# Splitting the dense attention's weights on ScalarE and VectorE in the middle of the last batch, and moving casts and gate copies of that batch to ScalarE

## The chip, the cores and the metric

One core of a Trainium2 chip runs the whole program. TensorE (PE) multiplies matrices, VectorE (DVE), ScalarE (ACT) and GpSimd (POOL) do everything else, and SyncE (SP) issues nearly all transfers. Each engine takes its instructions in the order in which they stand in its queue. The metric is device time in microseconds (us) of one execution, lower is better.

## The reference

Three layers follow each other for 4 batches of 576 positions: a sparse attention (8 heads of 64, half of them local, half strided), a gated feed-forward layer, and a dense causal attention with four experts of which two are used per position. The part around the change is the end of the second layer and the start of the third:

```
xk = mu_k * x + (1 - mu_k) * x_prev          # x_prev: x shifted by one position
xr = mu_r * x + (1 - mu_r) * x_prev
k  = max(xk @ w_k, 0)                         # 512 -> 1024
v  = (k * k) @ w_v                            # 1024 -> 512
r  = sigmoid(xr @ w_r)                        # 512 -> 512, the gate
y  = r * v
...
q, k, v = y @ wq[e], y @ wk[e], y @ wv[e]     # then causal softmax, @ wo[e], gated sum
```

## The kernel before, in words

Numbers are float32, and the products keep that precision by splitting. `split(src, h, l, he, le)` (L114) makes a rounded high part `h` on engine `he` and the rest `l = src - h` on engine `le`; a product is then three matmuls, high by high, high by low, low by high. The feed-forward layer of one batch, `p2_units(b)` (L451), works on two chunks of positions (320 and 256 columns). For a chunk, `prep` (L457) makes four pieces (one per 128 channels) of the mixed input for the gate (`xh_3_0`, `xl_3_0` of tag xh1) and four for the keys: POOL forms the difference `xd` (L472) once, DVE forms `xf = xd * mu + prev` (L479), and the split gives `xh` and `xl`. `mm3` (L536) makes four gate products `pr` of 12 matmuls and `evac` copies each from PSUM into the gate buffer `sg`; `mm1` (L500) makes eight key products `pk` of 12 matmuls, ACT does relu and square into `rf`, and a split gives `kk`; `mm2` (L554) makes four value products `pv` of 24 matmuls, and DVE multiplies each into `sg`, which is then written to memory (`x_spill`). One sigmoid over all of `sg` (L548) stands between the gate copies and the first of these multiplications.

`in_order` (L576) gives a batch's order: gate and key preparations and products of the first chunk, gate of the second, values of the first (`A["2"]`), then keys and values of the second (`Z["1"]`, `Z["2"]`). The batches overlap: while batch b is in its feed-forward layer, the sparse attention of batch b+1 is interleaved. The last batch (b = 3) has nothing to be interleaved with, so its feed-forward layer runs by itself between the last attention tiles and the dense attention. A list scheduler places the instructions of each engine within these dependences, so that an instruction can land earlier than its line in the text.

The PSUM tag `mm` has three banks that go round over `pr`, `pk` and `pv`. The fourth gate product needs the bank of the first, that is, the copy of the first into `sg`.

Just ahead of the last batch (L852 to L860) the four weights of the dense attention, 512 KB each (`wq`, `wk`, `wvg`, `wo`), are loaded one after the other into one staging buffer of tag `x2f`, and split: high part on ACT, low part on POOL. The buffer is free for the next load when POOL has made the low part. The same buffer then takes `x2f_0`, the first input chunk of the dense attention (L888), whose high part `x2h` is cast on ACT and whose low part `x2l` is made on DVE.

Of the kernel before, what the change touches and what calls it, by code (L numbers as in the profile page):

```python
# [7 lines left out]
F32 = mybir.dt.float32  # L8
# [8 lines left out]
P = 128  # L17
# [3 lines left out]
def interleave(main, side):  # L21

    tm = sum(c for c, _ in main) or 1.0
    ts_ = sum(c for c, _ in side) or 1.0
    im = is_ = 0
    am = as_ = 0.0
    while im < len(main) or is_ < len(side):
        if is_ < len(side) and (im >= len(main) or as_ / ts_ <= am / tm):  # L30
            c, f = side[is_]
            f()
            as_ += c
            is_ += 1
        else:
            c, f = main[im]
            f()
            am += c
            im += 1
# [3 lines left out]
def kernel(  # L43
# [19 lines left out]
    nc = tc.nc  # L63
    B, C, S = out.shape
# [3 lines left out]
    NKC = C // P  # L68
# [7 lines left out]
    CM = 320  # L76
# [11 lines left out]
    def ps_mm(name):  # L88
        return bank("mm", name, 3)
# [9 lines left out]
    def evac(dst, src, e=None):  # L99
        if e is None:  # L100
            flip["n"] += 1
            e = (nc.scalar, nc.vector)[flip["n"] % 2]
        if e is nc.scalar:
            nc.scalar.copy(dst, src)  # L104
        else:
            nc.vector.tensor_copy(dst, src)
# [7 lines left out]
    def split(src, h, l, he, le):  # L114

        if he is nc.scalar:
            nc.scalar.copy(h, src)  # L117
        else:
            he.tensor_copy(h, src)
        le.tensor_tensor(l, src, h.bitcast(F32), op=ALU.subtract)  # L120
# [10 lines left out]
    for nr in (7, 6):  # L131
        n = NN * nr
# [88 lines left out]
    sg = p2.tile([P, NKC, S], F32, tag="sg", name="sg", bufs=1)  # L221
# [229 lines left out]
    def p2_units(b):  # L451
        xT = xTs[b]
        parts = []
        for ci, (s0, N) in enumerate(CHUNKS1):
            st = {}

            def prep(which, kc, ci=ci, s0=s0, N=N, st=st, part=None):  # L457
                def f():
                    if part == 1:
                        st["low", which, kc]()  # L460
                        return
                    whole = b == 0 and which == 1
                    if kc == 0 and whole:
                        st["w"] = p2.tile([P, NKC, CM], F32, tag=("xh1", "xl1")[ci], name=f"xw{which}_{b}_{ci}", bufs=1)
                    elif kc == 0:
                        st["h", which] = p2.tile([P, NKC, CM], F32R, tag=f"xh{which}", name=f"xh{which}_{b}_{ci}", bufs=1)
                        st["l", which] = p2.tile([P, NKC, CM], F32R, tag=f"xl{which}", name=f"xl{which}_{b}_{ci}", bufs=1)
                    cur = xT[:, kc, 1 + s0:1 + s0 + N]
                    prv = xT[:, kc, s0:s0 + N]
                    if which == 1:  # L470
                        d = p2.tile([P, CM], F32, tag="xd", name=f"xd{b}_{ci}_{kc}", bufs=4)
                        (nc.vector if b == 0 else nc.gpsimd).tensor_tensor(d[:, :N], cur, prv, op=ALU.subtract)  # L472
                        st["d", kc] = d
                    d = st["d", kc]
                    if whole:
                        xf = st["w"][:, kc, :]
                    else:
                        xf = p2.tile([P, CM], F32, tag="xf", name=f"xf{which}_{b}_{ci}_{kc}")
                    nc.vector.scalar_tensor_tensor(  # L479
                        xf[:, :N], d[:, :N], mu[:, which, kc:kc + 1], prv, op0=ALU.mult, op1=ALU.add  # L480
                    )

                    he = nc.scalar if b == 0 else nc.vector
                    if whole:
                        return
                    h, l = st["h", which][:, kc, :N], st["l", which][:, kc, :N]
                    if part is None:
                        split(xf[:, :N], h, l, he, nc.vector)
                    else:
                        nc.scalar.copy(h, xf[:, :N])  # L490
                        st["low", which, kc] = lambda: nc.vector.tensor_tensor(
                            l, xf[:, :N], h.bitcast(F32), op=ALU.subtract
                        )
                return (0.0, f)

            U = {"r": [prep(1, kc) for kc in range(NKC)], "k": [prep(0, kc) for kc in range(NKC)]}
# [39 lines left out]
            def mm3(oc, ci=ci, s0=s0, N=N, st=st):  # L536
                def f():
                    xh, xl = st["h", 1], st["l", 1]
                    pm = ps_mm(f"pr{b}_{ci}_{oc}")
                    os_ = slice(oc * P, (oc + 1) * P)  # L540
                    for kc in range(NKC):
                        nc.tensor.matmul(pm[:, :N], wrh[:, kc, os_], xh[:, kc, :N], start=(kc == 0), stop=False)  # L542
                        nc.tensor.matmul(pm[:, :N], wrh[:, kc, os_], xl[:, kc, :N], start=False, stop=False)  # L543
                        nc.tensor.matmul(pm[:, :N], wrl[kc][:, os_], xh[:, kc, :N], start=False, stop=(kc == NKC - 1))  # L544
                    evac(sg[:, oc, s0:s0 + N], pm[:, :N], nc.vector)
                    if oc == NKC - 1 and ci == 1:

                        nc.scalar.activation(sg, sg, AF.Sigmoid)  # L548
                return (1.5 * N / 288, f)
# [26 lines left out]
    def in_order(parts):  # L576
        A, Z = parts
        return A["r"] + A["k"] + A["3"] + Z["r"] + A["1"] + Z["k"] + Z["3"] + A["2"] + Z["1"] + Z["2"]

    def behind(units):  # L580

        last = {}
        for i in nc.cur_bb.bb.instructions:
            last[i.engine] = i
        last = [last[e] for e in (nc.tensor.engine, nc.vector.engine, nc.scalar.engine, nc.sync.engine)]

        def wrap(f):
            def g():
                with ExitStack() as es:
                    for i in last:  # L590
                        es.enter_context(tc.issue_after(i))
                    f()
            return g
        return [(c, wrap(f)) for c, f in units]
# [21 lines left out]
    A, Z = p2_units(0)  # L616
# [202 lines left out]
    main = behind(A["2"][6:] + Z["1"])  # L819
# [20 lines left out]
    w3 = ctx.enter_context(tc.tile_pool(name="w3", bufs=1, side="right", reuse_waits="tile"))  # L840
    EP = E // 2
    wqh = w3.tile([P, NKC, E * D], F32R, tag="wqh", name="wqh")
    wql = w3.tile([P, NKC, E * D], F32R, tag="wql", name="wql")
    wkkh = w3.tile([P, NKC, E * D], F32R, tag="wkkh", name="wkkh")
    wkkl = w3.tile([P, NKC, E * D], F32R, tag="wkkl", name="wkkl")
    GV = E * D + E
    wvgh = w3.tile([P, NKC, GV], F32R, tag="wvgh", name="wvgh")
    wvgl = w3.tile([P, NKC, GV], F32R, tag="wvgl", name="wvgl")
    woh = w3.tile([P, EP, C], F32R, tag="woh", name="woh")
    wol = w3.tile([P, EP, C], F32R, tag="wol", name="wol")  # L850

    for src, h, l in ((wq, wqh, wql), (wk, wkkh, wkkl), (wvg, wvgh, wvgl)):  # L852
        n = src.shape[2]
        st = w3.tile([P, NKC, CM], F32, tag="x2f", name="w3st")
        nc.sync.dma_start(st[:, :, :n], src)
        split(st[:, :, :n], h, l, nc.scalar, nc.gpsimd)
    st = w3.tile([P, NKC, CM], F32, tag="x2f", name="wost")
    st = st.rearrange("p c n -> p (c n)")[:, :EP * C].rearrange("p (e n) -> p e n", e=EP)
    nc.sync.dma_start(st, wo)
    split(st, woh, wol, nc.scalar, nc.gpsimd)  # L860

    interleave(in_order(p2_units(B - 1)), [])
    r1.close()

    p3 = ctx.enter_context(tc.tile_pool(name="p3", bufs=2, reuse_waits="tile"))
# [234 lines left out]
    for b in range(B):  # L1100
# [4 lines left out]
        units = []  # L1105
# [103 lines left out]
```

## Time and profile before

| | |
|---|---|
| median of 3 runs | 582.27 us (582.23 to 584.96) |
| span of the profiled execution | 582.6 us |
| PE busy | 552.8 us, 95% of the span |
| DVE / ACT / POOL busy | 400.7 / 327.3 / 103.9 us |
| mean granted TensorE clock | 0.994 |
| chain that ended last | PE 75%, DVE 11%, ACT 5% |

The profiled execution has no time beside its span; that span stands 0.3 us over the median of the runs. In the profile a row of an instruction says when it started and how long it took. Matmuls are pipelined, so that the distance from start to start is their cost, not the duration in the row. The number in square brackets is the idle time of the engine just ahead, with what ended it.

### The profile page before, as it was taken

What the parts mean: (1) busy time and instruction counts of PE and PEld (TensorE: products, weight loads), DVE (VectorE), ACT (ScalarE), POOL (GpSimd) and SP (SyncE); (2) the same over time, 40 slices, a digit from 0 to 9 for tenths busy, and PEclk for the clock granted to TensorE, in tenths of its full rate; (3) what the DMA queues carried; (4) which work ended last, traced back from release to release, by engine and by line L of the source; (5) the groups of instructions that cost most, each with busy time, mean ns of one, the idle gap of its engine ahead of it and who ended that gap; (6) DMA issues with size and microseconds to landing.
All of it is one profiled execution on the core that took longest, in us unless ns stands there. A gap on an engine that the chain in (4) does not pass through costs nothing.

```text
span 582.6 us, 12015 instructions
## 1 busy us (share of the span) xinstructions
PE 552.8 (95%) x4408; PEld 500.2 (86%) x4408; DVE 400.7 (69%) x1366; ACT 327.3 (56%) x966; POOL 103.9 (18%) x151
## 2 busy tenths in 40 slices
PE   4889899989999999999997999999999999999987
PEld 3557788879999998999997999999988998898956
DVE  3897998768975476964467872336888874875862
ACT  4986878780345441445431352246775874775763
POOL 0000000101211021201114310076513142221000
PEclk9999999999999999999999899999999999999999
DMA  8872531323011223010202122054512250311102
GB/s 270 327 252 76 155 120 46 103 109 119 2 30 59 87 83 120 2 64 24 87 20 90 38 84 80 23 113 92 126 30 55 65 128 2 81 42 42 56 28 82
DMA packets 27519, 49.69 MB, mean 85 GB/s; under 512 B 3525, under 2 KB 22213, under 8 KB 26693
## 3 DMA queue, kind: packets, MB, share of 16 engines
q1 hardware_dynamic: 22340, 44.21, 22.9%
q0 software_dynamic: 5120, 4.72, 4.6%
q8 instruction: 34, 0.56, 0.4%
q14 instruction: 25, 0.20, 0.1%
HBM read 34.77 MB, written 9.44 MB: 76 GB/s over the span
## 4 chain that ended last, share of the span: by engine, by line
PE 75%; DVE 11%; ACT 5%; issue 2%; DVEq 0%; ACTq 0%
PE pk L506 6%; PE pv L563 6%; PE pk L507 5%; PE pk L508 5%; PE pv L565 5%; PE pv L564 5%; PE py L1064 4%; PE pt L1042 4%; PE pr L542 2%; PE s L1006 2%; PE pr L543 2%; PE pr L544 2%; PE pos L413 2%; PE s L1007 2%; PE pw L1080 2%
## 5 line engine op out<-in xcount | busy, mean ns | idle before, releaser
L506 PE MATMUL pk<-xh,wkh 128*128 128x320 f32 (+1 forms) x256 | 79.6, 312 | 3.8 <-ACT rf L510 2.7
L563 PE MATMUL pv<-kk,wvh 128*128 128x320 f32 (+1 forms) x256 | 76.4, 303 | 0.0
L507 PE MATMUL pk<-xl,wkh 128*128 128x320 f32 (+1 forms) x256 | 75.7, 296 | 0.0
L508 PE MATMUL pk<-xh,wkl 128*128 128x320 f32 (+1 forms) x256 | 75.6, 295 | 0.0
L564 PE MATMUL pv<-kk,wvh 128*128 128x320 f32 (+1 forms) x256 | 74.3, 293 | 0.0
L565 PE MATMUL pv<-kk,wvl 128*128 128x320 f32 (+1 forms) x256 | 73.9, 293 | 0.0
L510 ACT ACTIVATE rf<-pk 128x320 f32<-128x320 f32 (+1 forms) x64 | 25.9, 407 | 57.7 <-PE pk L508 45.0
L1017 ACT ACTIVATE pe<-pe,nm 128x384 f32<-128x384 f32 (+4 forms) x80 | 48.3, 606 | 12.4 <-DVE nm L1011 10.2
L506 PEld LDWEIGHTS pk<-xh,wkh 128*128 128x128 f32 x256 | 48.5, 190 | 7.8 <-ACT rf L510 3.8
L237 ACT ACTIVATE el<-el,nm 128x96 f32<-128x96 f32 x72 | 26.2, 366 | 45.1 <-DVE nm L232 44.6
L563 PEld LDWEIGHTS pv<-kk,wvh 128*128 128x128 f32 x256 | 47.7, 188 | 2.1 <-issue 0.3
L507 PEld LDWEIGHTS pk<-xl,wkh 128*128 128x128 f32 x256 | 48.6, 190 | 0.1
L508 PEld LDWEIGHTS pk<-xh,wkl 128*128 128x128 f32 x256 | 48.4, 189 | 0.1
L564 PEld LDWEIGHTS pv<-kk,wvh 128*128 128x128 f32 x256 | 47.9, 188 | 0.0
L565 PEld LDWEIGHTS pv<-kk,wvl 128*128 128x128 f32 x256 | 47.7, 188 | 0.1
L1011 DVE CUSTOM_DVE_ANT_0 pe<-s,mcau 128x384 f32<-128x384 f32 (+4 forms) x80 | 36.6, 479 | 10.4 <-PE s L1007 9.7
L104 ACT COPY aT<-pt 128x256 f32<-128x256 f32 (+3 forms) x96 | 33.4, 381 | 16.2 <-PE pt L1042 15.5
L1042 PE MATMUL pt<-ident,pe 128*128 128x128 f32 x240 | 37.9, 275 | 2.1 <-ACT aT L104 1.3
L568 DVE TENSOR_TENSOR sg<-pv,sg 128x320 f32<-128x320 f32 (+1 forms) x32 | 14.4, 457 | 32.8 <-PE pv L565 30.4
L237 ACT ACTIVATE es<-es,nm 108x108 f32<-108x108 f32 (+1 forms) x80 | 30.3, 383 | 8.8 <-DVE nm L232 8.8
L479 DVE SCALAR_TENSOR_TENSOR xf<-xd,mu,xT 128x320 f32<-128x320 f32 (+1 forms) x56 | 33.0, 600 | 3.3 <-POOL xd L472 3.3
L120 DVE TENSOR_TENSOR kk<-rf,kk 128x320 fp32r<-128x320 f32 (+1 forms) x64 | 31.1, 488 | 4.6 <-ACT kk L117 3.4
(162 smaller groups left out, 1565.0 us busy)
## 6 DMA issues: line engine op xcount, KB each, us to landing
qkv<-in_loc_dram SPq DMA_DIRECT2D x6, 1168.0 KB, 5.1
qkv<-in_strd_dram SPq DMA_DIRECT2D x6, 896.0 KB, 4.7
wraw<-in_w_k_dram SPq DMA_DIRECT2D x7, 512.0 KB, 6.5
qkv<-in_w_v_dram SPq DMA_DIRECT2D x5, 512.0 KB, 4.1
x_spill<-sg SPq DMA_DIRECT2D x16, 160.0 KB, 1.8
x2f<-x_spill SPq DMA_DIRECT2D x4, 640.0 KB, 4.5
out_dram<-ot SPq DMA_DIRECT2D x16, 160.0 KB, 1.8
wraw<-in_w_r_dram SPq DMA_DIRECT2D x4, 512.0 KB, 7.7
```

Source lines behind the costliest of these rows:

```text
L104: nc.scalar.copy(dst, src)
L237: nc.scalar.activation(eg, eg, AF.Exp, bias=nm[:np_, i:i + 1], scale=-1.0, accum_out=sm[:np_, i:i + 1],)
L479: nc.vector.scalar_tensor_tensor(xf[:, :N], d[:, :N], mu[:, which, kc:kc + 1], prv, op0=ALU.mult, op1=ALU.add)
L506: nc.tensor.matmul(pm[:, :N], wkh[:, kc, fs], xh[:, kc, :N], start=(kc == 0), stop=False)
L507: nc.tensor.matmul(pm[:, :N], wkh[:, kc, fs], xl[:, kc, :N], start=False, stop=False)
L508: nc.tensor.matmul(pm[:, :N], wkl[:, kc, fs], xh[:, kc, :N], start=False, stop=(kc == NKC - 1))
L563: nc.tensor.matmul(pm[:, :N], wvh[:, fc, os_], kh[:, :N], start=(fc == 0), stop=False)
L564: nc.tensor.matmul(pm[:, :N], wvh[:, fc, os_], kl[:, :N], start=False, stop=False)
L565: nc.tensor.matmul(pm[:, :N], wvl[:, fc, os_], kh[:, :N], start=False, stop=(fc == NFC - 1))
L1011: nc.vector.tensor_tensor_reduce(out=pe[:m, c0:c0 + n], in0=pm[:m, :n], in1=mask, scale=-0.125, scalar=(BIG if i == 0 else nm[:m, 2 * e:2 ...
L1017: nc.scalar.activation(pe[:m, :nk], pe[:m, :nk], AF.Exp, bias=last, scale=-1.0, accum_out=sm[:m, e:e + 1],)
L1042: nc.tensor.transpose(pt[:, kk * P:(kk + 1) * P], pe[:, c0:c0 + P], ident)
```

## The change

Three edits, all for the last batch. The high parts of the mixed inputs are cast on ACT and no longer on DVE. The gate products are copied out of PSUM by ACT and no longer by DVE. And the weights of the dense attention are loaded and split by a list of units (`w3_units`), interleaved with the last 24 units of the batch (`A["2"] + Z["1"] + Z["2"]`); each split comes in two halves, high on ACT and low on DVE, POOL has no part in it any more. The staging buffer is free for the next load when DVE has made the second half.

```diff
-                    he = nc.scalar if b == 0 else nc.vector
+                    he = nc.scalar if b in (0, B - 1) else nc.vector
...
-                    evac(sg[:, oc, s0:s0 + N], pm[:, :N], nc.vector)
+                    evac(sg[:, oc, s0:s0 + N], pm[:, :N], nc.scalar if b == B - 1 else nc.vector)
...
-    for src, h, l in ((wq, wqh, wql), (wk, wkkh, wkkl), (wvg, wvgh, wvgl)):
-        n = src.shape[2]
-        st = w3.tile([P, NKC, CM], F32, tag="x2f", name="w3st")
-        nc.sync.dma_start(st[:, :, :n], src)
-        split(st[:, :, :n], h, l, nc.scalar, nc.gpsimd)
...
-    interleave(in_order(p2_units(B - 1)), [])
+    def w3_units():
+        units = []
+        for src, h, l in ((wq, wqh, wql), (wk, wkkh, wkkl), (wvg, wvgh, wvgl), (wo, woh, wol)):
+            rows, n = src.shape[1:]
+            st = {}
+            def load(src=src, rows=rows, n=n, st=st):
+                t = w3.tile([P, NKC, CM], F32, tag="x2f", name="w3st")
+                st["w"] = t.rearrange("p c n -> p (c n)")[:, :rows * n].rearrange("p (c n) -> p c n", n=n)
+                nc.sync.dma_start(st["w"], src)
+            units.append((0.0, load))
+            for r in range(0, rows, rows // 2):
+                def part(r=r, rows=rows, h=h, l=l, st=st):
+                    rs = slice(r, r + rows // 2)
+                    split(st["w"][:, rs], h[:, rs], l[:, rs], nc.scalar, nc.vector)
+                units.append((1.0, part))
+        return units
+    A, Z = p2_units(B - 1)
+    main = in_order((A, Z))
+    n = len(main) - len(A["2"] + Z["1"] + Z["2"])
+    interleave(main[:n], [])
+    interleave(main[n:], w3_units())
```

The text puts the first load behind the gate products, but the scheduler still issues it where it stood, ahead of the last `x_spill` of batch 2 on SP. ACT's queue at the start of the last batch, before (`aTs` are the last transposes of the sparse attention, `rf_0_0` the first relu and square of the keys):

```order
284 L104 COPY aTs_3_0_3682<-pts_3_0_1_3687 126x252
285 L104 COPY aTs_3_1_3740<-pts_3_1_1_3746 108x324
286 L117 CAST wqh<-w3st 128x1024
287 L117 CAST wkkh<-w3st 128x1024
288 L510 ACTIVATE rf_0_0_3986<-pk_0_0_3973 128x320
```

And now, the same stretch of ACT's queue (`xh_3_0_3831` is the gate's input, `xh_3_0_3857` the keys'):

```order
289 L117 CAST xh_3_0_3831<-xf_3_0_3_3853 128x320
290 L117 CAST wqh<-w3st 128x512 x2
291 L117 CAST xh_3_0_3857<-xf_3_0_0_3859 128x320
292 L117 CAST xh_3_0_3857<-xf_3_0_1_3863 128x320
293 L104 COPY sg<-pr_0_0_3875 128x320
294 L104 COPY sg<-pr_0_1_3889 128x320
295 L104 COPY sg<-pr_0_2_3903 128x320
296 L117 CAST xh_3_0_3857<-xf_3_0_2_3867 128x320
297 L117 CAST xh_3_0_3857<-xf_3_0_3_3871 128x320
298 L117 CAST wkkh<-w3st 128x512 x2
299 L104 COPY sg<-pr_0_3_3917 128x320
```

The casts of the weights now stand among casts and copies that PE needs. DVE's queue at the same place, before:

```order
805 L479 SCALAR_TENSOR_TENSOR xf_3_0_1_3879<-xd_0_1_3855,mu,xT_2738 128x320
806 L479 SCALAR_TENSOR_TENSOR xf_3_0_2_3883<-xd_0_2_3861,mu,xT_2738 128x320
807 L119 CAST xh_3_0_3873<-xf_3_0_1_3879 128x320
808 L119 CAST xh_3_0_3873<-xf_3_0_2_3883 128x320
809 L120 TENSOR_TENSOR xl_3_0_3874<-xf_3_0_1_3879,xh_3_0_3873 128x320
810 L120 TENSOR_TENSOR xl_3_0_3874<-xf_3_0_2_3883,xh_3_0_3873 128x320
811 L106 COPY sg<-pr_0_0_3891 128x320
```

DVE's queue at that place now:

```order
798 L120 TENSOR_TENSOR xl_3_0_3832<-xf_3_0_3_3853,xh_3_0_3831 128x320
799 L120 TENSOR_TENSOR wql<-w3st,wqh 128x512
800 L479 SCALAR_TENSOR_TENSOR xf_3_0_1_3863<-xd_0_1_3839,mu,xT_2738 128x320
801 L120 TENSOR_TENSOR wql<-w3st,wqh 128x512
802 L120 TENSOR_TENSOR xl_3_0_3858<-xf_3_0_0_3859,xh_3_0_3857 128x320
803 L120 TENSOR_TENSOR xl_3_0_3858<-xf_3_0_1_3863,xh_3_0_3857 128x320
804 L479 SCALAR_TENSOR_TENSOR xf_3_0_2_3867<-xd_0_2_3845,mu,xT_2738 128x320
```

DVE no longer casts or copies here, and has the low halves of the weights in their place. The second place is ACT's queue around the second chunk's gate, before:

```order
303 L510 ACTIVATE rf_0_7_4116<-pk_0_7_4103 128x320
304 L117 CAST woh<-wost 128x1024
305 L514 ACTIVATE rf_0_7_4116<-rf_0_7_4116 128x320
306 L548 ACT_TABLE_LOAD
307 L548 ACTIVATE sg<-sg 128x2304
308 L117 CAST x2h_0_4578<-x2f_0_4576 128x1024
```

The same place now, with the four gate copies `sg<-pr_1_*` that DVE made before:

```order
323 L514 ACTIVATE rf_0_7_4100<-rf_0_7_4100 128x320
324 L104 COPY sg<-pr_1_0_4123 128x256
325 L117 CAST xh_3_1_4105<-xf_3_1_2_4115 128x256
326 L117 CAST x2h_0_4586<-x2f_0_4584 128x1024
327 L104 COPY sg<-pr_1_1_4137 128x256
328 L117 CAST xh_3_1_4105<-xf_3_1_3_4119 128x256
329 L104 COPY sg<-pr_1_2_4151 128x256
330 L104 COPY sg<-pr_1_3_4165 128x256
331 L548 ACT_TABLE_LOAD
332 L548 ACTIVATE sg<-sg 128x2304
```

`woh` has moved up ahead of `rf_0_6`, and `x2h_0`, which stood behind the sigmoid, stands ahead of the copy of `pr_1_1`.

## Rows read from the trace of the kernel before

**Rows 1.** Waits of PE from 48 us to the end: total, times, longest.

```profile
PE pr L542 <- DVE sg L106: 3.4, 1, 3.4
```

**Rows 2.** Busy time in stretches: length, PE, PEld, DVE, ACT, POOL, PEclk, DMA, GB/s.

```profile
315.00:320.00 5.00, 1.57 (x8) 1.31 (x7) 5.00 (x10) 0.45 (x1) 2.52 (x4) 0.79 0.33 105
320.00:325.00 5.00, 5.00 (x22) 5.00 (x21) 4.97 (x10) 0.60 (x1) 2.42 (x2) 0.53 0.09 13
```

**Rows 3.** Timeline of PE in the last batch: start, duration, instruction, idle before.

```profile
310.01 0.30 PE L542 MATMUL pr<-xh,wrh 128*128 128x320 f32 x1
...
315.14 0.30 PE L544 MATMUL pr<-xh,wrl 128*128 128x320 f32 x1
318.87 0.64 PE L542 MATMUL pr<-xh,wrh 128*128 128x320 f32 x1 [3.43 <-DVE sg L106]
...
324.64 0.35 PE L506 MATMUL pk<-xh,wkh 128*128 128x320 f32 x1
...
337.44 0.28 PE L542 MATMUL pr<-xh,wrh 128*128 128x256 f32 x1
...
343.09 0.36 PE L563 MATMUL pv<-kk,wvh 128*128 128x320 f32 x1
```

**Rows 4.** Chain that ended last, 295 to 390 us: start, length, what.

```profile
313.24 3.07 DVE xf L479 x2
...
318.34 0.49 DVE sg L106
```

**Rows 5.** Timeline of POOL, 300 to 350 us.

```profile
311.63 0.62 POOL L472 TENSOR_TENSOR xd<-xT 128x256 f32<-128x256 f32 x1 [1.68 <-DVE xf L479]
312.88 2.62 POOL L120 TENSOR_TENSOR wql<-w3st,wqh 128x1024 fp32r<-128x1024 f32 x1 [0.62 <-ACT wqh L117]
```

**Rows 6.** Timeline of DVE, 300 to 350 us.

```profile
310.55 1.00 DVE L479 SCALAR_TENSOR_TENSOR xf<-xd,mu,xT 128x320 f32<-128x320 f32 x2
...
313.17 3.14 DVE L479 SCALAR_TENSOR_TENSOR xf<-xd,mu,xT 128x320 f32<-128x320 f32 x2
```

**Rows 7.** Timeline of ACT, 300 to 350 us.

```profile
311.76 1.05 ACT L117 CAST wqh<-w3st 128x1024 fp32r<-128x1024 f32 x1 [8.43 <-DMA w3st<-in_wq_dram]
...
344.75 2.13 ACT L548 ACTIVATE sg<-sg 128x2304 f32<-128x2304 f32 x1 [3.84 <-DVE sg L106]
346.79 1.04 ACT L117 CAST x2h<-x2f 128x1024 fp32r<-128x1024 f32 x1
```

**Rows 8.** Groups by line and shape: count, busy us, mean ns.

```profile
L184 ACT CAST wvh<-wf 128x512 fp32r<-128x512 f32 x8 | 5.0, 620 | 3.5 <-DVE wf L177 3.5
...
L490 ACT CAST xh<-xf 128x320 fp32r<-128x320 f32 x4 | 1.9, 463 | 0.5 <-DVE xf L479 0.5
L532 ACT COPY sg<-pr 128x320 f32<-128x320 f32 x4 | 1.6, 435 | 2.4 <-PE pr L526 2.4
...
L120 DVE TENSOR_TENSOR wrl0t<-wrw,wrh 128x512 fp32r<-128x512 f32 x1 | 0.7, 681 | 0.0
```

**Rows 9.** Timeline of SP, 300 to 350 us.

```profile
307.35 0.67 SPq L855 DMA_DIRECT2D w3st<-in_wq_dram  x1
...
315.53 0.55 SPq L855 DMA_DIRECT2D w3st<-in_wk_dram  x1
...
334.52 0.34 SPq L859 DMA_DIRECT2D wost<-in_wo_dram  x1
```

**Rows 10.** Waits of SP, 296 to 350 us: total, times, longest.

```profile
SPq L889 <- DMA wost<-in_wo_dram: 3.3, 1, 3.3
```

**Rows 11.** DMA issues: count, KB each, median us to landing.

```profile
wraw<-in_w_k_dram SPq DMA_DIRECT2D x7, 512.0 KB, 6.5
...
x2f<-x_spill SPq DMA_DIRECT2D x4, 512.0 KB, 5.0
...
w3st<-in_wq_dram SPq DMA_DIRECT2D x1, 512.0 KB, 4.3
w3st<-in_wk_dram SPq DMA_DIRECT2D x1, 512.0 KB, 4.0
```

More of the change, by code (lines that the diff above doesn't have):

```diff
@@ L850 @@
     wol = w3.tile([P, EP, C], F32R, tag="wol", name="wol")
-    for src, h, l in ((wq, wqh, wql), (wk, wkkh, wkkl), (wvg, wvgh, wvgl)):
-        n = src.shape[2]
-        st = w3.tile([P, NKC, CM], F32, tag="x2f", name="w3st")
-        nc.sync.dma_start(st[:, :, :n], src)
-        split(st[:, :, :n], h, l, nc.scalar, nc.gpsimd)
[L857 to L860, printed above, removed]
-    interleave(in_order(p2_units(B - 1)), [])
+    def w3_units():
[19 more added lines that the diff above has]
+    interleave(main[n:], w3_units())
     r1.close()
```

## The prediction

> **What bounds the kernel now.** I read the waits of PE first, since PE is busy for 95% of the span. From 48 us on one wait stands out: 3.4 us of a gate product for a copy that DVE makes into `sg` [rows 1]. The busy time by stretches shows where it lies and that it costs more than itself: between 315 and 320 us PE issued 8 matmuls, between 320 and 325 only 22, with a granted clock of 0.53 in the second [rows 2]. So I went to PE's timeline. The 36 matmuls of the first three gate products run from 310.01 to 315.14, 0.147 us each from start to start; then PE stands until 318.87; then 21 matmuls take until 324.64, 0.275 us each with the first, which is the 1.2 GHz level of the clock [rows 3]. Idle 315.29 to 318.87 is 3.58 us; the 21 slow matmuls took 5.77 us where full clock takes 21 x 0.147 = 3.09, a loss of 2.68. Together **6.3 us**. Nothing else is lost there: from 324.64 to 343.09, where the first value product starts, the starts follow each other at 0.147 us (320 columns) and, from 337.44, at (343.09 - 337.44) / 48 = 0.118 us (256 columns) [rows 3].
>
> What held the copy is in the chain that ended last: it leaves PE for DVE, two mixes of 3.07 us together, casts, then the copy at 318.34 [rows 4]. Two such mixes took 1.00 us at 310.55; the slow pair at 313.17 [rows 6] ends 0.8 us after POOL's `wql`, which ran from 312.88 to 315.50 [rows 5]: DVE did not get on beside it. The copy of the first gate product, ready at about 314.9, stood in DVE's queue behind all this.
>
> **Edit 1 and 2, casts and gate copies to ACT.** DVE loses 16 casts and 8 copies in this batch, ACT gets them at 0.46 us (cast) and 0.44 us (copy) for 320 columns [rows 8]. ACT has room: it idled 8.43 us ahead of `wqh` [rows 7]. Three of the casts lie under batch 2, where PE never waited for long; I count them at nothing, and without that cover they would cost 3 x 0.46 = 1.4 us at most. The path at the start of the batch becomes: last mix of the gate input at 311.1, cast on ACT 311.2, `wqh` in two halves (landed as before, 311.76 [rows 7]) until 312.95, two key casts until 314.3, and then the copy of the first gate product at 314.9, when PE has finished it. It ends at 315.35 and the fourth product starts 0.1 us late instead of 3.58. The remaining key pieces come off DVE at about 318.0; PE needs the last at 319.7. No gap, so no slow clock: up to here the whole 6.3 us are won. PE would reach the first value product at 310.0 + 144 x 0.147 + 48 x 0.118 = 336.8, against 343.09.
>
> **Edit 3, the weights.** POOL loses four low parts of about 2.6 us [rows 5], and DVE is rid of waits behind them. DVE gets eight halves at 0.68 us (the nearest row, same operation and size [rows 8]), ACT eight at 0.62 instead of four at 1.05 [rows 7, 8]. The price is that ACT and DVE now wait for transfers with PE's work queued behind. Behind `wkkh` on ACT stands the copy of `pr_0_3`, behind `wvgh` the relu of `pk_0_2`, behind `woh` that of `pk_0_6`, and behind `x2h_0` the copy of `pr_1_1`, whose bank the first value product takes.
>
> The chain of loads: `wq` was issued at 307.35 and stays there behind the spills [rows 9]. The second half of `wql` ends on DVE at 314.45 (first half 312.7 after `wqh` and after POOL's last `xd` at 312.25 [rows 5]; a mix between; second half 313.75). `wk` is then issued at 314.5, 1.0 us earlier than before [rows 9]. One round is: load, cast 0.62, low halves 0.60 and 0.69, three hand-overs of 0.05, that is load + 2.06; in the third weight's round another 0.40 for a low part of `kk` between the halves. Three rounds later, with loads of 3.7, `x2f_0` is issued at 314.5 + 3 x 3.7 + 6.6 = 332.2.
>
> The load is the disputed size. Three loads with 1 KB pieces took 4.0 to 4.3 us [rows 11]; the one that already had the new form (128 x 1024), `wo`, was issued at 334.52 [rows 9], its issue took 0.34, and SP then waited 3.3 us for it [rows 10], so it took 3.64. I take 3.7 for the weights, near the row of the same form, and 4.0 for `x2f_0`, which keeps 1 KB pieces and has the size of `wk`; the bounds are 3.4 and 4.3 for the one, 3.7 and 5.0 (median of its form, beside other transfers) for the other [rows 11]. Then `x2f_0` lands at 336.2, `x2h_0` holds ACT for 0.95, the copy of `pr_1_1` ends at 337.6, and the first value product starts there: a new wait of **0.8 us**. The three earlier places stay covered: `wkkh` leaves the copy of `pr_0_3` at 319.3 (needed 320.6), `wvgh` the relu at 325.1 (bank needed 325.9, 0.4 spare after the relu), `woh` its relu at 331.3 (needed 332.6).
>
> The Trainium skill, "DMA: Bandwidth & Descriptors", section "Anatomy of one DMA — SWDGE (gpsimd) path", fits a transfer as about 2.0 us plus bytes over 436 GB/s, by which 512 KB would take an estimated 3.2 us. That fit is for another issue path than SP's, and the rows above are slower than it; by 3.2 us the new wait would be gone and the sum would be rival (a)'s.
>
> **Behind the gate.** The sigmoid takes 2.13 us [rows 7] after a table load, ends near 342, and the first multiplication follows; the bank it frees is needed only by the fourth value product, near 348. After that the order on PE is the same as before and PE was full, so the gain is carried to the end.
>
> **Sum.** 6.3 - 0.8 = 5.5 us off the profiled 582.6, which stands 0.3 over the median; on the median, 582.27 - 5.5 = **576.8 us**.
>
> **Rivals.** (a) *The loads hide fully*: at 3.4 and 3.7 us `x2f_0` comes in time, gain 6.3, 576.0. For it: the newer form's one row is already the fastest; against: no load here took less than 3.6. (b) *Loads as the older rows, 4.3 and 5.0*: `x2f_0` lands 2 x 1.4 later in all, the relu of `pk_0_2` costs PE 0.9, the wait at the value product is 2.6, gain 2.7, 579.6. For it three rows of four, against it their other form. (c) *The new wait drops the clock*: PE's one long stand was followed by the low level [rows 2, 3]; if 0.8 us were followed by it too, 2.7 us go, 579.5. Against: the other waits of PE after 48 us, all shorter, show no low clock in the profile. (d) *Slower*: ACT's queue stands at `wvgh`, `woh` and `x2h_0` while a load is under way. Each microsecond of load beyond 4.0 costs four (four loads in a row); at 5.2 us per load the gain is gone, at 6.5, what the `w_k` loads took [rows 11], the first value product starts at 348.5, 5.4 us late: 587.7. For it: the row of 6.5; against: those loads ran early in the kernel beside others, here the transfers of the last batch are alone. (e) *The change doesn't do what it says*, DVE still being late for the fourth gate product, because its eight weight halves (5.5 us) replace what it lost: then about 582. Against: no gate copy stands in its queue any more.
>
> **How the numbers follow.** Forecast with its neighbourhood (576.2 to 578.6) 0.55; (a) 0.17; (b) 0.09; (c) 0.08; (d) 0.06; (e) 0.05. The range runs from full hiding, with 0.2 us to spare, to the edge of (b) and (c): 575.8 to 580.0. About 0.5% (2.9 us) is what a measurement of this kernel can tell from no change: faster means under 579.4. Forecast, (a) and a third of (b) and (c) are faster: 0.78; the rest of these with (e) are the same: 0.15; (d), with a little from (e), slower: 0.07.
>
> **What would show it.** Right: the wait of `pr` for `sg` of 3.4 us is gone and no stretch between 310 and 345 us has a granted clock under 1; the fourth gate product starts near 315.4; the first value product near 337.6, waiting on ACT's copy `sg<-pr`; POOL has no `L120` there; loads of 3.6 to 3.8 us. Wrong: a wait of over 1 us at `pk` for `rf` (loads longer than taken), a low clock after 336 us, or a gain that is there at 343 us and gone by the end of the trace.

## The result and the profile after

The changed kernel took 577.79 us (median of 4 runs, 576.82 to 579.01) where the kernel before took 582.86 beside it (4 runs, 582.23 to 584.96): ratio 0.990, 95% interval 0.987 to 0.993. It is faster, and the time lies 1.0 us over the 576.8 that was forecast and within the range. The profiled execution has a span of 576.3 us against 582.6; its time was 578.21.

The busy time by stretches (length, PE, PEld, DVE, ACT, POOL, PEclk, DMA, GB/s) where rows 2 had 8 and 22 matmuls:

```profile
315.00:320.00 5.00, 5.00 (x34) 4.81 (x34) 4.93 (x10) 3.88 (x10) 1.61 (x2) 1.00 0.37 108
320.00:325.00 5.00, 5.00 (x37) 5.00 (x36) 4.81 (x13) 3.69 (x10) 0.00 (x0) 1.00 0.34 107
```

PE is busy throughout at full clock, and between 305 and 345 us it has no wait at all: that of [rows 1] is gone, and nothing has taken its place. PE's timeline, to be held against [rows 3]:

```profile
309.98 0.30 PE L542 MATMUL pr<-xh,wrh 128*128 128x320 f32 x1
...
315.11 0.30 PE L544 MATMUL pr<-xh,wrl 128*128 128x320 f32 x1
315.34 0.42 PE L542 MATMUL pr<-xh,wrh 128*128 128x320 f32 x1
...
336.83 0.28 PE L544 MATMUL pr<-xh,wrl 128*128 128x256 f32 x1
336.95 0.31 PE L563 MATMUL pv<-kk,wvh 128*128 128x320 f32 x1
```

The fourth gate product starts 0.08 us late, not 3.58. From the first gate product to the first value product it takes 26.97 us, before it took 33.08: **6.1 us** gained, of 6.3 that the spans differ by. From there to the end of the span it is 239.4 us now and 239.5 before, so the gain is carried to the end. I use this distance (first `pr` to first `pv`) for all kernels below; it doesn't hang on what happened earlier in an execution.

ACT's timeline in the last batch, the counterpart of [rows 7]:

```profile
311.46 1.14 ACT L117 CAST wqh<-w3st 128x512 fp32r<-128x512 f32 x2
...
314.87 1.08 ACT L104 COPY sg<-pr 128x320 f32<-128x320 f32 x3 [0.81 <-PE pr L544]
...
317.78 1.14 ACT L117 CAST wkkh<-w3st 128x512 fp32r<-128x512 f32 x2 [0.97 <-DMA w3st<-in_wk_dram]
...
335.17 1.05 ACT L117 CAST x2h<-x2f 128x1024 fp32r<-128x1024 f32 x1 [1.32 <-DMA x2f<-x_spill]
336.13 0.36 ACT L104 COPY sg<-pr 128x256 f32<-128x256 f32 x1
...
338.83 2.13 ACT L548 ACTIVATE sg<-sg 128x2304 f32<-128x2304 f32 x1
```

The gate copies now wait for PE, no longer PE for them. The last lines are the place of the forecast's new wait: ACT stands 1.32 us for `x2f_0`, then the copy of `pr_1_1` ends at 336.49, and PE wants its bank only at 336.95. There are 0.46 us to spare, where I had forecast 0.8 us of wait. SP's timeline gives the chain of loads that leads there (for [rows 9]):

```profile
307.32 0.42 SPq L862 DMA_DIRECT2D w3st<-in_wq_dram  x1
...
314.19 0.33 SPq L862 DMA_DIRECT2D w3st<-in_wk_dram  x1
319.98 0.33 SPq L862 DMA_DIRECT2D w3st<-in_wvg_dram  x1
325.86 0.33 SPq L862 DMA_DIRECT2D w3st<-in_wo_dram  x1
331.44 6.44 SPq L905 DMA_DIRECT2D x2f<-x_spill  x2
```

ACT's casts of these weights start at 317.78, 323.46 and 329.47, that of `x2f_0` at 335.17. That makes loads of 3.6 (`wk`), 3.5 (`wvg`), 3.6 (`wo`) and 3.7 us (`x2f_0`). POOL and DVE, for [rows 5, 6]:

```profile
313.71 0.93 POOL L472 TENSOR_TENSOR xd<-xT 128x256 f32<-128x256 f32 x1 [1.16 <-DVE xf L479]
```

```profile
310.52 1.00 DVE L479 SCALAR_TENSOR_TENSOR xf<-xd,mu,xT 128x320 f32<-128x320 f32 x2
...
313.48 0.68 DVE L120 TENSOR_TENSOR wql<-w3st,wqh 128x512 fp32r<-128x512 f32 x1
...
315.31 1.00 DVE L479 SCALAR_TENSOR_TENSOR xf<-xd,mu,xT 128x320 f32<-128x320 f32 x2
```

No pair of mixes takes 3.14 us any more.

### The profile page after: what moved, and what is told of

It is laid out like the page before. It is cut to its first block, busy times and chain, and to the rows that moved or that the text cites. A ratio compares the mean times of both kernels' runs of the same rounds, so it can differ in the third digit from the quotient of the medians.

```text
span 576.3 us, 12027 instructions
## 1 busy us (share of the span) xinstructions
PE 550.2 (95%) x4408; PEld 497.8 (86%) x4408; DVE 391.2 (68%) x1350; ACT 336.2 (58%) x994; POOL 94.8 (16%) x147
## 4 chain that ended last, share of the span: by engine, by line
PE 76%; DVE 10%; ACT 5%; issue 2%; DVEq 0%; ACTq 0%
PE pk L506 6%; PE pv L563 6%; PE pk L507 5%; PE pk L508 5%; PE pv L565 5%; PE pv L564 5%; PE py L1080 4%; PE pt L1058 4%; PE pr L542 2%; PE pr L543 2%; PE pr L544 2%; PE s L1022 2%; PE pos L413 2%; PE s L1023 2%; PE pw L1096 2%; PE ss L382 2%
## 5 line engine op out<-in xcount | busy, mean ns | idle before, releaser
L1022 PE MATMUL s<-KH,Q 128*128 128x288 f32 (+4 forms) x96 | 31.9, 342 | 1.1 <-DVE nm L1027 1.1
```

Source lines behind the costliest of these rows:

```text
L1022: nc.tensor.matmul(pm[:m, :n], qs, KH[:, e, c0:c0 + n], start=True, stop=False)
```

## The experiments

Four kernels carry parts of the change, three change a duration that was in dispute, and the kernels before and after were profiled again. A stand is a stretch in which PE stands idle and waits. Theory: POOL's low parts hold DVE, the late copy of the first gate product follows from that, and the loads decide whether ACT is late later on. Rivals: DVE simply had too much to do; the change gains by the copies' move to ACT alone; ACT's waits for loads give it back. First the whole change (`e0_whole_change`, the kernel after, unedited) and its parts.

> The whole change again, timed beside the partial ones on one chip. Theory (the copy of the first gate product stood in VectorE's queue behind work that GpSimd's wql held up; the change frees that queue, and its loads land in 3.4 to 3.7 us, in time for x2h_0): fourth gate product 0.1 us late, no low clock, first value product near 337.0, about 6.2 us less than before in the trace and 0.99 of its time. Rival (the gain is mostly scatter between runs): the ratio's interval reaches 1.

Measured: 578.17 us against 583.52, ratio 0.990 [0.988, 0.993]; 26.97 us from first `pr` to first `pv`, no wait there, as in the first profile.

`e1_moves_only`, edits 1 and 2 without the weights:

```diff
-                    he = nc.scalar if b == 0 else nc.vector
+                    he = nc.scalar if b in (0, B - 1) else nc.vector
...
-                    evac(sg[:, oc, s0:s0 + N], pm[:, :N], nc.vector)
+                    evac(sg[:, oc, s0:s0 + N], pm[:, :N], nc.scalar if b == B - 1 else nc.vector)
```

> Casts and gate copies of the last batch on ScalarE, weights still split ahead of the batch with the low parts on GpSimd. Theory: GpSimd's wql (2.6 us) still holds VectorE's mixes, the key casts on ScalarE wait for these mixes, and the copy of the first gate product stands behind the third key cast in ScalarE's queue: fourth gate product near 318.5, low clock after it as before, gain under 1 us (582.0 of 582.5, ratio 0.997 to 1.0). Rival (taking casts and copies off VectorE is what counts): the gate product starts near 315.4, gain 5 to 6 us, ratio 0.99.

Measured: 581.97 us, ratio 0.996 [0.994, 0.998]. The place and the mechanism are as expected (`wql` on POOL, DVE held, the third key cast on ACT late, behind it the copy), but the stand was 2.24 us and no low clock followed it. So the gain was not under 1 us: it is 1.55 us between the medians (583.52 and 581.97) and 2.3 by the ratio.

`e2_weights_only`, edit 3 alone, that is, the loop ahead of the last batch replaced by `w3_units`:

```diff
-    for src, h, l in ((wq, wqh, wql), (wk, wkkh, wkkl), (wvg, wvgh, wvgl)):
...
+    interleave(main[:n], [])
+    interleave(main[n:], w3_units())
```

> Weights split in halves on ScalarE and VectorE among the batch, casts and gate copies still on VectorE. Theory: without wql on GpSimd the copy of the first gate product comes up in VectorE's queue near 316.3, PE stands about 1.5 us there and 0.6 more at the keys' fourth piece (behind wkkl, which waits for its load), no low clock if a stand of 1.5 us doesn't bring it: gain about 4 us (578.5, ratio 0.993). With a low clock 1.4. Rival (VectorE's own work is the bound, which grows by eight halves, 5.5 us): no gain or a loss, fourth gate product after 318.

Measured: 578.64 us, ratio 0.992 [0.989, 0.994]. PE stands 0.98 us at the fourth gate product, whose copy DVE still makes, and has no other wait; 1.5 us there and 0.6 at the keys were expected. Edit 3 alone takes 33.08 down to 28.26 us, 4.8 of the 6.1.

`e3_copies_only`, edit 2 alone, the second pair of lines of `e1_moves_only`'s diff:

> Only the gate copies of the last batch on ScalarE; casts on VectorE, weights as before. Theory: the copy stands behind wqh alone on ScalarE, fourth gate product near 315.4; VectorE stays held by GpSimd's wql and wkkl, so PE waits later: 0.4 us for the keys' fourth piece near 320 and 1.8 us for a relu behind VectorE's kk near 327. Gain about 4 us (578.5, ratio 0.993), no low clock. Rival (the copy is all that matters): no later wait, gain 6 us, ratio 0.99.

Measured: 580.41 us, ratio 0.995 [0.993, 0.997]. No wait at the fourth gate product, but one of 1.39 us at 327.20, as expected, and one of 0.37 at 337.36 in the second chunk's gate. The gain is 3.1 us at the medians, not 4. What makes the product at 327.20 late is again a pair on DVE that POOL holds, now `wkkl`:

```profile
320.23 2.96 DVE L120 TENSOR_TENSOR xl<-xf,xh 128x256 fp32r<-128x256 f32 x2
```

```profile
320.31 2.60 POOL L120 TENSOR_TENSOR wkkl<-w3st,wkkh 128x1024 fp32r<-128x1024 f32 x1 [1.33 <-ACT wkkh L117]
```

So the move of the copies to ACT alone keeps a part of the gain: the hold moves on to the next product that needs DVE.

`e4_casts_only` is the first pair alone.

> Before with the casts of the last batch's mixed inputs on ScalarE; the gate copies stay on VectorE, the weights' low parts on GpSimd. Theory (GpSimd's low part of wq holds VectorE, and the copy of the first gate product stands in VectorE's queue behind the held mixes): the copy is still made on VectorE near 317.5 us, PE stands 2.2 to 3.3 us at the fourth gate product, ended by VectorE's copy into sg, and the gain is 0.4 to 2 us (ratio 0.996 to 0.999). Rival (the casts in VectorE's queue are what delays the copy): with them gone PE's stand falls under 1.5 us and the gain is 3 us or more (ratio under 0.995).

Measured: 582.24 us against 584.27, ratio 0.997 [0.995, 0.999]; PE stands 2.28 us at the fourth gate product, for DVE's copy. The casts had gone from DVE's queue, and the copy was late all the same:

```profile
313.42 3.34 DVE L120 TENSOR_TENSOR xl<-xf,xh 128x320 fp32r<-128x320 f32 x2
...
317.61 0.88 DVE L106 COPY sg<-pr 128x320 f32<-128x320 f32 x2
```

`e5_low_on_vector` is the decisive test. One word of the kernel before differs, in two places (L856, and L860 for `wo`); VectorE gets more to do:

```diff
-        split(st[:, :, :n], h, l, nc.scalar, nc.gpsimd)
+        split(st[:, :, :n], h, l, nc.scalar, nc.vector)
```

> Before with one word changed: the low parts of the dense attention's four weights are made whole on VectorE, not on GpSimd. Loads, casts and copies stay as they were. Theory (GpSimd's long two-input operations hold VectorE, the weights' place in the text is secondary): the two mixes that took 3.14 us take about 1 us, the fourth gate product starts about 0.95 us late in place of 3.58, no low clock follows, and the gain is 3.5 to 5 us (ratio 0.991 to 0.994), a rest being lost where VectorE has a 1.3 us low part ahead of a piece of the keys. Rival (VectorE simply has too much to do there, and 2.7 us more of weights on it makes it later): no gain or a loss, ratio 1.0 or more.

Measured: 579.85 us, ratio 0.992 [0.991, 0.994]; 28.54 us from `pr` to `pv`. DVE's row shows the low part whole among the mixes, with nothing held, and the copies at 314.66:

```profile
312.00 0.54 DVE L479 SCALAR_TENSOR_TENSOR xf<-xd,mu,xT 128x320 f32<-128x320 f32 x1
312.46 1.21 DVE L120 TENSOR_TENSOR wql<-w3st,wqh 128x1024 fp32r<-128x1024 f32 x1
...
314.66 0.87 DVE L106 COPY sg<-pr 128x320 f32<-128x320 f32 x2
```

```profile
315.19 0.41 PE L542 MATMUL pr<-xh,wrh 128*128 128x320 f32 x1 [0.91 <-DVE sg L106]
```

The rival falls: DVE had room for the work. What POOL took 2.4 to 2.7 us for takes DVE 1.21 to 1.25, and the wait for the keys that I expected behind `wkkl` did not come. POOL's hold of DVE is the cause of 4.5 of the 6.1 us that lie between the first profiles (33.08 to 28.54); in time it is 4.4 us at the medians (584.27 to 579.85).

Then the loads. `e6_loads_twice` adds a second, equal load behind each of the four:

```diff
                 nc.sync.dma_start(st["w"], src)
+                nc.sync.dma_start(st["w"], src)
```

> After, with each of the four weights loaded twice, one load behind the other, so that every weight's data comes about 3 us later. The list scheduler sees the longer load and puts the casts further back in ScalarE's queue. Theory (what a long load costs is set by what stands behind the cast in ScalarE's queue, and only the first cast, wqh, still has gate copies behind it): the fourth gate product starts about 1 us late, the rest is covered, the kernel stays 4.5 to 5.5 us faster than before (ratio 0.990 to 0.9925). Rival (the prediction's rival d, each microsecond of load costs four): 3 us more per load takes 12 us less what slack there is, at least 4.7 us of loss, and the kernel is no faster than before (ratio 0.999 or more).

Measured: 579.48 us, ratio 0.992 [0.990, 0.993]; two waits of PE, 0.66 and 0.53 us. The first is the expected one, behind `wqh`; the second, a gate product of the second chunk that waits for ACT's last relu behind `wvgh`, was not expected:

```profile
313.42 1.14 ACT L117 CAST wqh<-w3st 128x512 fp32r<-128x512 f32 x2 [0.24 <-DMA w3st<-in_wq_dram]
314.46 1.07 ACT L104 COPY sg<-pr 128x320 f32<-128x320 f32 x3
```

Doubled loads cost 1.5 us of the 6.1, not 12. This says nothing on the slope in the order of the kernel after: seeing the longer load, the scheduler placed `wkkh` behind the second relu of the keys, `wvgh` just ahead of the last one, and `woh` and `x2h_0` behind the sigmoid. It shows only that rival (d)'s four microseconds per microsecond does not hold where the scheduler knows of the longer loads; in the order of the kernel after, no weight's load over 4.1 us was tried.

`e7_old_form_loads` keeps the order of every engine and gives `wq`, `wk` and `wvg` the staging form of the kernel before (128 x 4 x 256):

```diff
                 st["w"] = t.rearrange("p c n -> p (c n)")[:, :rows * n].rearrange("p (c n) -> p c n", n=n)
+                if rows == NKC:
+                    st["w"] = t[:, :, :n]
```

> After, with wq, wk and wvg staged in the form that the kernel before used (128 x 4 x 256 with a gap behind each piece in place of 128 x 1024 in one stretch); the order of the instructions on every engine is the same as in after. Theory (the form sets the load's length, 4.0 to 4.3 against 3.4 to 3.7 us, and the chain of loads ends at x2h_0 with 0.46 us to spare): the loads take about 4.0 us, x2f_0 lands about 1.1 us later, PE waits 0.5 to 0.9 us for the copy of pr_1_1 ahead of the first value product, and the time is 0.5 to 1 us over after's (ratio to before about 0.991 to 0.993). Rival (the form does not matter, the loads are short because nothing runs beside them): loads of 3.4 to 3.7 us, no wait, and the time of after.

Measured: 579.84 us, ratio 0.992 [0.990, 0.994]. The loads took 4.1 us as expected, yet the wait at the first value product was 1.58 us, twice what I had said. `x2f_0` itself had taken 5.05 us (issued 330.91), and the stretches show how:

```profile
333.00:334.00 1.00, 1.00 (x11) 1.00 (x10) 1.00 (x4) 0.32 (x1) 0.00 (x0) 1.00 0.87 303
334.00:335.00 1.00, 1.00 (x11) 1.00 (x10) 0.24 (x1) 0.00 (x0) 0.00 (x0) 1.00 0.05 7
335.00:336.00 1.00, 0.75 (x7) 0.54 (x5) 0.00 (x0) 0.04 (x1) 0.00 (x0) 1.00 0.03 7
```

```profile
335.96 1.04 ACT L117 CAST x2h<-x2f 128x1024 fp32r<-128x1024 f32 x1 [2.65 <-DMA x2f<-x_spill]
```

```profile
337.33 0.41 PE L563 MATMUL pv<-kk,wvh 128*128 128x320 f32 x1 [1.58 <-ACT sg L104]
```

Nearly all had landed by 334.0; a rest at 7 GB/s held the cast for 1.9 us. So I ran the old form again, beside the kernel after.

> After with wq, wk and wvg staged in the old form, a second time. The first look had loads of 4.1 us and a wait of 1.6 us ahead of the first value product, of which x2f_0 itself, with 5.0 us against 3.7 in after, made 1.3. If that long x2f_0 belongs to the form, the wait is 1.6 us again; if it was a chance of that execution, x2f_0 takes 3.5 to 3.8 us and the wait is 0.3 to 0.7 us. In time: 0.4 to 1 us over after, ratio to before 0.991 to 0.9925.

> After, unchanged, beside the former on the same chip: the same profile as in its first two looks, no wait of PE between 305 and 345 us, loads of 3.4 to 3.7 us and x2f_0 of 3.6 to 3.8 us; ratio to before 0.9895 to 0.991.

Measured: 577.76 us, ratio 0.990 [0.988, 0.993], and 578.13 us, ratio 0.991 [0.988, 0.993]. In the second profile of the old form the weights took 4.0 to 4.1 us, `x2f_0` 3.55, and PE lost 0.2 us (27.16 against 26.97), less than the 0.3 to 0.7 expected. So the long `x2f_0` does not come with the form every time (the two profiles were also taken on different chips); without it the form's 0.5 us per load costs next to nothing at this spare. The kernel after showed no wait for the third time.

Last, the kernel before, twice, unedited, since `e1_moves_only` and `e4_casts_only` had shown no low clock behind their stands.

> The kernel before, unchanged, profiled a second time. Kernels with a stand of 2.2 to 2.3 us at the fourth gate product (moves only, casts only) showed no low clock behind it, the profile of before showed one behind 3.58 us. If the stand brings the low clock by its length, this profile again has about 3.5 us of stand and a granted clock near 0.5 between 320 and 325 us, and 2.5 to 2.7 us lost with it. If the low level of that profile was an event of its own, the clock is 1.00 there and the span about 2.7 us shorter, 580.

> The kernel before, unchanged, a third profile, for the same question: low clock behind a stand of 3.5 us every time, or only sometimes. Three profiles with it would make it a part of the stand's price, one without it a chance; then the gain of the change is 3.5 us in some executions and 6.2 in others.

Measured: 584.10 us (span 581.3) and 583.08 us (span 580.5). The stand is the same in both, 3.49 and 3.48 us, though here it was the pair of `xl` parts that POOL's `wql` held (3.08 us in both), not the pair of mixes. The row of 320 to 325 us, in the second profile and in the third:

```profile
320.00:325.00 5.00, 5.00 (x25) 5.00 (x25) 5.00 (x11) 0.00 (x0) 1.83 (x1) 0.67 0.32 96
```

```profile
320.00:325.00 5.00, 5.00 (x36) 5.00 (x35) 5.00 (x11) 1.48 (x4) 1.81 (x1) 1.00 0.32 97
```

There are 21 matmuls at the 1.2 GHz level in the second and none in the third. And the third has a wait that the first two lacked (waits of PE, 300 to 350 us):

```profile
PE pr L542 <- DVE sg L106: 3.5, 1, 3.5
PE pv L563 <- DVE sg L106: 1.3, 1, 1.3
```

At full clock PE came to the first value product earlier than DVE had copied `pr_1_1`, because POOL's `wol` held DVE there:

```profile
337.26 0.42 DVE L106 COPY sg<-pr 128x256 f32<-128x256 f32 x1
337.59 2.30 DVE L479 SCALAR_TENSOR_TENSOR xf<-xd,mu,xT 128x256 f32<-128x256 f32 x1
```

```profile
337.11 2.50 POOL L120 TENSOR_TENSOR wol<-wost,woh 128x1024 fp32r<-128x1024 f32 x1 [4.70 <-ACT woh L117]
```

All together (stand at the fourth gate product; what else PE lost by waits; first `pr` to first `pv`; ratio to the kernel before with its interval):

| kernel | stand | else | `pr` to `pv` | ratio |
|---|---|---|---|---|
| before, first profile | 3.43 | low clock | 33.08 | 1 |
| before, second profile | 3.49 | low clock | 33.03 | 1 |
| before, third profile | 3.48 | 1.29 | 32.12 | 1 |
| casts only | 2.28 | 0.46 | 29.94 | 0.997 [0.995, 0.999] |
| moves only | 2.24 | 0 | 29.27 | 0.996 [0.994, 0.998] |
| copies only | 0 | 1.39, 0.37 | 29.94 | 0.995 [0.993, 0.997] |
| low parts on VectorE | 0.91 | 0.17 | 28.54 | 0.992 [0.991, 0.994] |
| weights only | 0.98 | 0 | 28.26 | 0.992 [0.989, 0.994] |
| loads twice | 0.66 | 0.53 | 28.49 | 0.992 [0.990, 0.993] |
| old form, first profile | 0 | 1.58 | 28.86 | 0.992 [0.990, 0.994] |
| old form, second profile | 0 | 0 | 27.16 | 0.990 [0.988, 0.993] |
| whole change | 0 | 0 | 26.97 | 0.990 [0.988, 0.993] |

The waits are idle times of PE; counted from start to start each costs about 0.15 us more. With the copies alone PE also lost some 0.6 us in short gaps at the keys' pieces (317.06 and 319.63) that the profile lists as no wait. The parts do not add up, since each shortens the same stand.

## Why the prediction was right, and where it was off

- **What held PE** was named rightly, and the one-word kernel shows it: with POOL's low parts on DVE, 4.5 of the 6.1 us are won. The Trainium skill, "SBUF — State Buffer", section "SBUF: two separate sides", states that GpSimd and VectorE share a pair of ports which one of them takes for a whole instruction, and that a VectorE operation with two SBUF inputs is shut out by a GpSimd operation that reads SBUF. The traces agree: 2.30 us for a mix beside `wol` that took 0.48 just before, while the copy out of PSUM at 337.26 ran through in its 0.42.
- **Fourth gate product at 315.4, full clock**: 315.34, and 1.00 in every stretch from 310 to 350 us.
- **Behind the gate**: the sigmoid ran until 340.96 (forecast near 342), the first multiplication started at 340.99, and PE had no wait up to the fourth value product.
- **The mis-sized term is the new wait of 0.8 us.** It rested on loads of 3.7 us for the weights and 4.0 for `x2f_0`. `wk` was issued at 314.19, 0.31 earlier than worked out; the three rounds took 17.25 us, not 17.7, since the loads took 3.6, 3.5 and 3.6; and `x2f_0` took 3.73. That is 0.31 + 0.45 + 0.27 = 1.03 us, the difference between 336.2 and 335.17. The mechanism, ACT waiting for `x2f_0` with the copy of `pr_1_1` behind it, is there and 0.46 us from showing; in the first profile of the old form it showed, with 1.58. Rival (a) describes the trace of the change better than the forecast did.
- **Rival (b)'s loads** of 4.0 to 4.3 us are what the old form gives. (b) put 3.6 us on them together with an `x2f_0` of 5.0; they cost 0.2 us when `x2f_0` took 3.55, and 1.9 (28.86 against 26.97) when it took 5.05, and the relu of `pk_0_2` cost PE nothing in either. **Rival (d)** did not come: no single one of these loads was longer than 5.1 us in any profile. **Rivals (c) and (e)** did not come.
- **The clock term was sized from one execution.** The 2.68 us were lost in two of three profiles of the kernel before. Where they were not, 1.29 us of wait appeared at the first value product, so that the low clock cost 0.9 us net (33.05 against 32.12), and the change gains 5.2 instead of 6.1 us. The other runs of the kernel before allow no closer figure: of 47 timed beside the experiments, 15 have a mean granted clock of 0.991 to 0.994 (that of the first two profiles is 0.994) and a median span of 582.4 us, 15 have 0.997 or more and 580.8, and a mean does not say where the low level lay. The prediction's "nothing else is lost there" was true only while PE was slow.
- **The base was off the other way.** I took the profiled execution for one near the median (span 0.3 us above it). In the thirteen later profiles the time stands 1.8 to 2.9 us above the span, so that the execution of 582.6 us of span took about 584.4 to 585.5, like the slowest run shown (584.96). Its losses were subtracted from a median of 582.27. That is most of why the median came out at 577.79 though PE lost less than forecast. In time the change gains 5.1 to 5.4 us at the medians of three comparisons, near the 5.2 that the profile without the low clock gives and under the 6.1 with it. That the forecast gain of 5.5 us lies so near is partly luck: 0.8 us was taken off for a wait that did not come, and 2.7 was counted in full for a low clock that comes in some executions and costs less.

What brings the low level stays open: stands of 3.48 and 3.49 us on the same code had full clock behind one and the low level behind the other, and stands of 2.24 and 2.28 had full clock in the one profile of each.

## What to carry to other kernels

When a short operation of VectorE takes three times its usual time, look at what GpSimd runs in the same microseconds before counting VectorE as overloaded: giving VectorE GpSimd's part can make both earlier. When a stall is removed, look for the next late instruction at the pace that PE will then have, since a slow clock hides waits behind it. And set the losses of a profiled execution against that execution's own time, not against the median of others.

## What the runs showed of the hardware that was not expected

- A cast, with one input, is held as well: a cast of `rf` that takes 0.32 us took 2.30 beside POOL's `wvgl` in the third profile of the kernel before:

```profile
330.30 2.30 DVE L119 CAST kk<-rf 128x320 fp32r<-128x320 f32 x1 [0.79 <-ACT rf L514]
```

```profile
329.97 2.44 POOL L120 TENSOR_TENSOR wvgl<-w3st,wvgh 128x1040 fp32r<-128x1040 f32 x1 [8.16 <-ACT wvgh L117]
```

- The weights, 512 KB each (`wvg` 520) and issued by SP, took 3.4 to 3.8 us staged in one stretch per partition, and 4.0 to 4.3 in four pieces with a gap behind each, once 5.1 (`wk`, with the copies alone). `x2f_0`, in such pieces too, took 3.5 to 3.8 in six profiles, 4.1 with the doubled loads and once 5.05, so the pieces alone do not make the difference.
- That one `x2f_0` had a tail: its last bytes came at 7 GB/s for 1.9 us. The cause was not tried.
